# Four loads reordered, six dummy matmuls fewer and an uneven last output tile in a fused attention and expert kernel

## The chip, the core and the metric

The kernel runs on one core of a Trainium2 chip. A core has five engines with instruction streams of their own: TensorE (PE, the matrix multiplier; PEld is its weight load), VectorE (DVE), ScalarE (ACT), GpSimd (POOL) and SyncE (SP). They meet through semaphores. Transfers between device memory (HBM) and on-chip memory (SBUF) are issued by SP, ACT or POOL and carried out by 16 DMA engines, which all issuers share. Matmuls write to PSUM, a small accumulator memory in banks, from which DVE and ACT read.

The metric is the device time of one execution in microseconds (us). The profile is one execution recorded by the hardware; its *span* runs from the first to the last instruction.

## What is computed

Causal attention over 4 batches, 8 heads, 768 positions and head size 64, in which heads 0, 2 and 6 ("retrieval") see all earlier positions and the other five ("streaming") see the first 4 positions and a window of the last 64. Its output, 3072 rows of 512, goes through four experts, whose results are summed with normalised weights:

```python
scores = q @ k.T / 8;  a = softmax(where(mask[h], scores, -1e9))
x = (a @ v).transpose(0, 2, 1, 3).reshape(3072, 512)
p = probs / (probs.sum(-1, keepdims=True) + 1e-9)
out = sum(p[:, e:e+1] * (relu(x @ w1[e]) @ w2[e]) for e in range(4))
```

w1 is 4 x 512 x 1024 and w2 is 4 x 1024 x 512. All inputs are float32 in HBM; POOL's transfers turn them into float16 on the way.

## The kernel before, in words

**Groups and units.** The 3072 rows are cut into 8 groups of 384 (batch `b`, half `c`; `g = 2b + c`). For each group there is an attention (`attention(b, c)`, line 495) and four expert *units* (`moe_steps`, line 880). Unit (g, e) has two layers: layer 1 (line 895) multiplies w1(e) by the transposed attention output `xT[g]`, 8 x 4 matmuls of 384 columns, each finished block going through ReLU on ACT (line 908) into `hs`; layer 2 (line 919) multiplies `hs` by w2(e), 3 x 8 matmuls of 512 columns into `pO`, which DVE scales by `p_sb` and adds up in `acc` (lines 931 and 935). After the fourth expert SP writes `acc` out (line 940).

**Order of PE's work.** The order of the instructions on PE, DVE, ACT, POOL and SP is written out by hand. Attention of group 0 comes first, by itself; then the units of group g run with the attention steps of group g + 1 strewn among them, by planned costs (loop at line 968). An engine takes its instructions in that order; one that waits holds up all behind it.

**Group 0's attention** (lines 778 to 803). Head by head: transposes of q and k, scores (line 614), exp on ACT (line 632), and the values step. For streaming heads that is `values(h)` (line 709): its matmuls (line 726) take the loaded values `vS` as weights; then Ln and Exp on ACT (lines 744, 754 or 759) make the reciprocal of the softmax sum, and DVE multiplies it into `xT` (line 749). Heads 3 and 4 share one Exp. For retrieval heads `values_r` (line 647) is followed by DVE operations (lines 675 to 682) and, for head 6, by `x_transposes(6)` on PE (line 703) and a copy on DVE (line 707). The last steps are `values(5)`, `x_transposes(6)`, `values(7)`. Of `xT`'s four row blocks, block 1 holds heads 1 and 5, block 2 heads 2 and 6, block 3 heads 3 and 7; the first four blocks of layer 1 of unit (0, 0) use row blocks 0, 2 and 1 first and block 3 last (lines 886 to 907).

**Dummies.** `warm_up` (line 386) issues matmuls on a constant tile whose result nobody reads. In `values` (line 719) there are 4, 4, 6 and 10 of them, of 256 columns, ahead of heads 3, 4, 5 and 7.

**POOL's loads.** Every transfer that changes float32 to float16 is issued by POOL, in its program's order. The order up to line 483 is: values of group 0's heads, w1(0), values of heads 5 and 7, w2(0), w1(1), k and q of group 1 (`load_triples`), w2(1), retrieval values of group 1, w1(2), two of its streaming heads, w2(2), the other three, w1(3), w2(3). In between stand one-element copies, `landed(x)` (line 458): POOL waits there until x has arrived in SBUF. One w1(e) is two transfers of 512 KB and one w2(e) one of 1024 KB (sizes as they arrive); a head's values are 48 KB, k and q of group 1 are 384 KB each. POOL's transfers use eight semaphores in turn, so each also waits for the landing of the one eight before it. After w2(3), POOL clears some tiles and loads k (`kRr`, `kSr`), q and v of group 2.

**SP's queue.** For the groups from 2 on, q and k are transposed by DMA, issued by SP in `dma_transposes` (line 248), in order behind other work of SP: the first output (line 940), the copies of the first keys (lines 243, 244), three transposes of q (line 253), then `kR<-kRr` and `kS<-kSr` (line 259). PE's scores of group 2 need these.

**The last tile.** The last 128 rows of the last unit are written by `last_tile` (line 857) in two halves of 256 columns: 8 matmuls (line 863), one DVE operation (line 870) and one output transfer (line 875) each, the first transfer by SP, the second by ACT.

Of the kernel before, what the change touches and what calls it, by code (L numbers as in the profile page):

```python
# [17 lines left out]
def kernel(  # L18
# [33 lines left out]
    nc = tc.nc  # L52
    P = 128
    B, H, S, D = q.shape
    E, DM, F = moe_w1.shape
# [94 lines left out]
    def half(u):  # L150
        return slice(u * D, (u + 1) * D)
# [5 lines left out]
    def own_v(h):  # L157
        return half(PLACE[h][1])
# [10 lines left out]
    def v_tiles(b, c, h):  # L169

        if RETR[h]:
            return vR[b % 2][:, 3 * c : 3 * c + 3, RH.index(h), :]
        if b:
            return windows(vSf, c)[:, :, SH.index(h), :]
        return vS[:, c, :, SH.index(h), :]

    def v_tile(b, c, h, t):

        if b:
            return v_tiles(b, c, h)[:, t, :]  # L180
        return v_tiles(b, t // TC, h)[:, t % TC, :]
# [4 lines left out]
    def rows_of(x, b, h, c):  # L186
        return x[b, h, c * CH : (c + 1) * CH, :].rearrange("(j p) d -> p j d", p=P)

    def tiles_of(x, b, h, c):
        return x[b, h, c * CH : (c + 1) * CH, :].rearrange("(t r) d -> r t d", r=TK)  # L190

    def windows_of(x, b, h, c):

        assert b > 0
        first = ((b * H + h) * S + c * CH - WO) * D
        return bass.AP(x.tensor, x.offset + first, [[D, P], [WQ * D, WT], [1, D]])
# [13 lines left out]
    def load_triples(x, dst, b, c):  # L210

        gp.dma_start(
            out=dst.rearrange("p h j d -> p h (j d)"),
            in_=x[b, :, c * CH : (c + 1) * CH, :].rearrange(
                "h (p j) d -> p h (j d)", j=3
            ),
        )
# [47 lines left out]
    def load_v(b, c, heads):  # L265
        for h in heads:
            t = v_tiles(b, c, h)
            if RETR[h]:
                gp.dma_start(out=t[:, :, 0:D], in_=rows_of(v, b, h, c))  # L269
            elif b:  # L270
                gp.dma_start(  # L271
                    out=t[:, :, own_v(h)], in_=windows_of(v, b, h, c)
                )
            else:
                gp.dma_start(  # L275
                    out=t[R0:P, :, own_v(h)],
                    in_=tiles_of(v, b, h, c),
                )
# [18 lines left out]
    def load_w1(e, f0, f1):  # L297
        x = moe_w1[e].rearrange("(u c d) f -> u d c f", u=2, c=DMP)
        for u in range(2):
            gp.dma_start(  # L300
                out=w1sb[half(u), e * DMP : (e + 1) * DMP, f0:f1],
                in_=x[u, :, :, f0:f1],
            )

    def load_w2(e):
        gp.dma_start(
            out=w2sb[:, e * FTP : (e + 1) * FTP, :],
            in_=moe_w2[e].rearrange("(fo fi) d -> fi fo d", fi=P),
        )
# [41 lines left out]
    for h in range(H):  # L351
        if h == 2:
            nc.sync.dma_start(
                out=v_s32, in_=v[0, :, 0:NS, :].rearrange("h r d -> r h d")
# [13 lines left out]
        eng = nc.scalar if h < HP else nc.sync  # L368
        eng.dma_start(out=q32[:, :, h, :], in_=rows_of(q, 0, h, 0))
    nc.sync.dma_start(  # L370
        out=probs, in_=moe_domain_probs.rearrange("(t p) e -> p t e", p=P)
# [14 lines left out]
    def warm_up(ps, n, cols):  # L386
        for _ in range(n):
            nc.tensor.matmul(
                out=ps[:, 0:cols], lhsT=warm[:, 0:P], rhs=warm[:, 0:cols],
                start=True, stop=True,  # L390
            )
# [13 lines left out]
    def mask_s(x, n, keep, drop):  # L405

        gp.memset(x, keep)
        gp.affine_select(
            out=x, in_=x, compare_op=ALU.is_ge, fill=drop,
            base=R0, pattern=[[0, n], [1, TQ]], channel_multiplier=-1,  # L410
        )
        gp.affine_select(
            out=x, in_=x, compare_op=ALU.is_ge, fill=drop,
            base=NW - 1 - R0, pattern=[[0, n], [-1, TQ]], channel_multiplier=1,
        )
        gp.memset(x[0:R0, :, :], drop)
        gp.memset(x[0:NS, :, 0:TK], keep)
        gp.affine_select(
            out=x[0:NS, 0, 0:TK], in_=x[0:NS, 0, 0:TK], compare_op=ALU.is_ge,
            fill=drop, base=-NW, pattern=[[1, TK]], channel_multiplier=-1,  # L420
        )
# [23 lines left out]

    mask_c(bC, 0.0, -60000.0)
    mask_s(bS[:, 0:2, :], 2, 0.0, -60000.0)
    load_v(0, 0, [2, 1, 3, 4, 6])
    load_w1(0, 0, F)
    load_v(0, 0, [5, 7])  # L450
    load_w2(0)
    zero(gp, kR[0][:, 1, :, :, :])
    zero(gp, kS[:, 1, :, :, :].rearrange("p t s x -> p s t x"))
# [4 lines left out]
    def landed(x):  # L458

        gp.tensor_copy(out=seen, in_=x)  # L460
# [4 lines left out]
    def w2_of(e):  # L465
        return w2sb[0:1, e * FTP, 0:1]
# [2 lines left out]
    landed(w1_of(0))  # L469
    load_triples(k, k16, 0, 1)  # L470
    load_triples(q, qt16, 0, 1)
    landed(w2_of(0))
    load_w2(1)
    landed(qt16[0:1, 0, 0, 0:1])
    load_v(0, 1, RH)
    load_w1(2, 0, F)
    landed(w2_of(1))
    load_v(0, 1, SH[:2])
    load_w2(2)
# [12 lines left out]
    def mm_ns(cols):  # L492
        return cols / 2.4 + 2.5

    def attention(b, c):
# [213 lines left out]
        def values(h):  # L709
            if RETR[h]:  # L710
                yield from values_r(h)
                return
            ct, u = PLACE[h]
            if first and u == 1:
                ps = pO.tile([P, 512], FP32, name="pO", bufs=2)
            else:
                ps = pV.tile([P, 512], FP32, name="pV", bufs=2)
            if first:
                warm_up(ps, {3: 4, 4: 4, 5: 6, 7: 10}.get(h, 0), 256)
            work = []  # L720
            for es, parts in es_of[h]:
                for t, o, q0, nq in parts:
                    work.append((es, t, o, q0, nq))
            ns = 0
            for n, (es, t, o, q0, nq) in enumerate(work):
                nc.tensor.matmul(  # L726
                    out=ps[:, q0 : q0 + nq],
                    lhsT=v_tile(b, c, h, t),
                    rhs=es[:, o : o + nq],
                    start=(n == 0),  # L730
                    stop=(n == len(work) - 1),
                    skip_group_check=True,
                )
                ns += mm_ns(nq)
                if ns > 300 and n < len(work) - 1:
                    yield ns
                    ns = 0

            r, o = half(u), half(1 - u)
            pair = first and h in (3, 4)  # L740
            if not pair or u == 0:
                rc_of[0] = att.tile([P, CH], FP32, name="rc", bufs=4)
            rc = rc_of[0]
            nc.scalar.activation(  # L744
                out=rc[r, :], in_=ps[o, 0:CH], func=AF.Ln, bias=eps[o, :]
            )

            def scale(r=r, ps=ps):
                nc.vector.tensor_tensor(  # L749
                    out=xT[g][r, ct, :], in0=ps[r, 0:CH], in1=rc[r, :], op=ALU.mult  # L750
                )

            if not pair:
                nc.scalar.activation(out=rc[r, :], in_=rc[r, :], func=AF.Exp, scale=-1.0)  # L754
                later(scale)
            elif u == 0:
                scale_of[0] = scale
            else:
                nc.scalar.activation(out=rc, in_=rc, func=AF.Exp, scale=-1.0)
                later(scale_of[0])  # L760
                later(scale)

            yield ns + (600.0 if g == 1 else 0.0)
# [14 lines left out]
        if first:  # L778
# [8 lines left out]
            sink_row(5)  # L787
            sink_row(7)
            yield from both(scores(1), values(0))
            yield from transposes(2)  # L790
            yield from both(scores(3), values(2))
            x_transposes(0)
            yield from scores(4)
# [55 lines left out]
    def later(op):  # L849
        behind.append((clock[0] + LAG, op))  # L850
# [5 lines left out]

    def last_tile(e, nt, hs, acc):

        for n, eng in enumerate((nc.sync, nc.scalar)):
            cols = slice(n * DM // 2, (n + 1) * DM // 2)  # L860
            ps = pV.tile([P, 512], FP32, name="pV", bufs=2)
            for ft in range(FTP):
                nc.tensor.matmul(
                    out=ps[:, 0 : DM // 2],
                    lhsT=hs[:, ft, 2 * P : 3 * P],
                    rhs=w2sb[:, e * FTP + ft, cols],
                    start=(ft == 0),
                    stop=(ft == FTP - 1),
                )
            nc.vector.scalar_tensor_tensor(  # L870
                out=acc[:, cols], in0=ps[:, 0 : DM // 2],
                scalar=p_sb[:, nt, e : e + 1], in1=acc[:, cols],
                op0=ALU.mult, op1=ALU.add,
            )
            eng.dma_start(out=out[nt * P : (nt + 1) * P, cols], in_=acc[:, cols])


    acc = {}
# [157 lines left out]
```

The softmax here doesn't subtract the row's maximum and nothing guards it: scores larger than these inputs give would overflow.

## Time and profile before

| What | us |
|---|---|
| median of 4 executions | 399.31 |
| lowest and highest | 398.95, 399.71 |
| the profiled execution | 399.71 |
| its span | 397.9 |
| PE busy | 388.9 (98% of the span) |
| ACT busy | 219.2 (55%) |
| DVE busy | 156.4 (39%) |
| POOL busy | 143.7 (36%) |
| granted PE clock, mean | 1.000 |

A timeline row gives the start in us from the span's start, the time taken, the engine, the line of the kernel, the operation, what it writes and reads, and how many instructions are merged in the row; in square brackets stands the idle time of the engine just before it and what ended that. Rows of the waits say who waited for whom: us in total, how often, the longest. PE's matmuls overlap, so a row's time is longer than the distance to the next row; where costs are summed, that distance is used.

### The profile page before, as it was taken

To read this page: it belongs to the slowest core of one execution; us is meant where nothing else is said; L and a number is where in the kernel's file an instruction comes from. 1 tells how busy PE (TensorE), PEld (TensorE's weight loads), DVE (VectorE), ACT (ScalarE), POOL (GpSimd) and SP (SyncE) were. 2 spreads that over 40 slices of the span, in tenths; PEclk is the share of its full clock that TensorE was granted. 3 is DMA by queue.
4 is the path that set the end of the run, shared out by engine and by line. 5 is a ranking of instruction groups with operands and counts; after the bars stand their busy time and mean duration, and the time that the engine had idled before them with its cause. 6 is when DMAs were issued, how large, how long until landed. Compare 5 with 4: busy or idle time off the path is not lost.

```text
span 397.9 us, 7140 instructions
## 1 busy us (share of the span) xinstructions
PE 388.9 (98%) x2829; PEld 221.7 (56%) x2829; DVE 156.4 (39%) x344; ACT 219.2 (55%) x468; POOL 143.7 (36%) x184
## 2 busy tenths in 40 slices
PE   8899999989999999999999999999999999999996
PEld 5754556545555555555555555555555555655553
DVE  7734765324432334433342333433443223432222
ACT  3754569434766546655674446845564456853331
POOL 8833795808916905910039202950000000000000
PEclk9999999999999999999999999999999999999999
DMA  9999999999999999980779949990472000020002
GB/s 169 160 208 193 182 197 163 134 182 142 111 168 182 112 150 119 131 108 11 127 86 174 73 88 127 106 159 12 80 120 82 3 12 0 12 79 2 0 2 80
DMA packets 166133, 42.23 MB, mean 106 GB/s; under 512 B 156396, under 2 KB 161108, under 8 KB 166100
## 3 DMA queue, kind: packets, MB, share of 16 engines
q0 software_dynamic: 102656, 20.98, 62.8%
q1 hardware_dynamic: 61700, 20.27, 27.1%
q10 hardware_dynamic: 1744, 0.52, 0.6%
q8 instruction: 22, 0.36, 0.4%
q14 instruction: 11, 0.09, 0.1%
HBM read 43.57 MB, written 6.29 MB: 125 GB/s over the span
## 4 chain that ended last, share of the span: by engine, by line
PE 77%; DMA 15%; POOL 6%; issue 1%; DVE 0%; POOLq 0%
PE pA L895 35%; PE pO L919 35%; DMA w1sb<-in_moe_w_dram 4%; DMA w2sb<-in_moe_w_dram 4%; PE pA L614 4%; DMA q<-in_q_dram 3%; DMA kR<-kRr 2%; PE pV L726 1%; PE pV L662 1%; POOL vR L269 1%; DMA vS<-in_v_dram 1%; POOL q L201 1%; POOL w1sb L300 1%; POOL vS L275 1%; POOL vS L326 0%
## 5 line engine op out<-in xcount | busy, mean ns | idle before, releaser
L895 PE MATMUL pA<-xT,w1sb 128*128 128x384 f16 x1024 | 185.9, 326 | 0.1
L919 PE MATMUL pO<-w2sb,hs 128*128 128x512 f16 x760 | 179.0, 379 | 0.7 <-DMA w2sb<-in_moe_w_dram 0.7
L908 ACT ACTIVATE hs<-pA 128x384 f16<-128x384 f32 x256 | 122.0, 492 | 94.8 <-PE pA L895 89.5
L895 PEld LDWEIGHTS <-w1sb 128*128 128x128 f16 x1024 | 95.8, 98 | 59.6 <-issue 0.5
L919 PEld LDWEIGHTS <-hs 128*128 128x128 f16 x760 | 70.8, 98 | 73.7 <-DMA w2sb<-in_moe_w_dram 1.1
L632 ACT ACTIVATE es<-pA 128x384 f16<-128x384 f32 (+2 forms) x122 | 60.0, 511 | 54.5 <-PE pA L614 53.2
L935 DVE SCALAR_TENSOR_TENSOR acc<-pO,p_sb,acc 128x512 f32<-128x512 f32 x71 | 53.3, 750 | 71.7 <-PE pO L919 71.3
L227 POOL DMA_DIRECT2D kSr<-in_k_dram x30 | 30.1, 1007 | 31.5 <-DMA kS<-kSr 21.9
L223 POOL DMA_DIRECT2D kRr<-in_k_dram x18 | 14.1, 786 | 69.8 <-DMA kR<-kRr 69.7
L749 DVE TENSOR_TENSOR xT<-pV,rc 64x384 f16<-64x384 f32 x37 | 20.5, 554 | 32.0 <-ACT rc L754 24.3
L271 POOL DMA_DIRECT2D vS<-in_v_dram x30 | 30.5, 1026 | 0.2 <-DMA q<-in_q_dram 0.2
L931 DVE TENSOR_SCALAR acc<-pO,p_sb 128x512 f32<-128x512 f32 x24 | 18.0, 751 | 28.8 <-PE pO L919 28.6
L636 DVE TENSOR_TENSOR es<-es,mC 128x256 f16<-128x256 f16 (+1 forms) x42 | 10.9, 259 | 46.3 <-ACT es L632 45.3
L744 ACT ACTIVATE rc<-pV,eps 64x384 f32<-64x384 f32 x37 | 21.3, 576 | 12.0 <-PE pV L726 11.5
L614 PE MATMUL pA<-qT,kR 128*128 128x384 f16 (+2 forms) x120 | 24.5, 278 | 1.7 <-DMA kR<-kRr 1.1
L754 ACT ACTIVATE rc<-rc 64x384 f32<-64x384 f32 x38 | 19.8, 521 | 1.2
L269 POOL DMA_DIRECT2D vR<-in_v_dram x24 | 19.3, 804 | 0.4 <-issue 0.3
L614 PEld LDWEIGHTS <-kR 128*128 128x128 f16 x120 | 11.4, 98 | 11.7 <-DMA kR<-kRr 1.5
L636 DVE TENSOR_TENSOR es<-es,mW 128x384 f16<-128x384 f16 x30 | 10.7, 358 | 16.9 <-ACT es L632 16.8
L662 PEld LDWEIGHTS <-es 128*128 128x128 f16 x252 | 13.2, 97 | 7.2 <-ACT es L632 0.9
L726 PEld LDWEIGHTS <-vS 128*128 128x128 f16 x255 | 13.4, 98 | 6.8 <-DMA vS<-in_v_dram 1.2
L614 PEld LDWEIGHTS <-kS 128*128 128x128 f16 x255 | 13.3, 98 | 6.6 <-DVE kS L556 0.2
(102 smaller groups left out, 190.6 us busy)
## 6 DMA issues: line engine op xcount, KB each, us to landing
out_dram<-acc SPq DMA_DIRECT2D x23, 256.0 KB
w1sb<-in_moe_w_dram POOLq DMA_DIRECT2D x8, 512.0 KB, 9.7
w2sb<-in_moe_w_dram POOLq DMA_DIRECT2D x4, 1024.0 KB, 13.2
kSr<-in_k_dram POOLq DMA_DIRECT2D x30, 112.0 KB, 3.8
vS<-in_v_dram POOLq DMA_DIRECT2D x30, 112.0 KB, 5.7
q<-in_q_dram POOLq DMA_DIRECT2D x18, 128.0 KB, 4.6
vR<-in_v_dram POOLq DMA_DIRECT2D x24, 48.0 KB, 5.0
kRr<-in_k_dram POOLq DMA_DIRECT2D x18, 48.0 KB, 3.8
```

What stands on the lines that cost most here:

```text
L227: gp.dma_start(out=kSr[:, :, SH.index(h), own(h)], in_=windows_of(k, b, h, c),)
L269: gp.dma_start(out=t[:, :, 0:D], in_=rows_of(v, b, h, c))
L271: gp.dma_start(out=t[:, :, own_v(h)], in_=windows_of(v, b, h, c))
L614: nc.tensor.matmul(out=ps[:, o : o + nq], lhsT=key_tile(b, c, h, t), rhs=qTs[b, c][:, hp, q0 : q0 + nq], start=(n == 0 or not first), stop ...
L632: nc.scalar.activation(out=es[:, 0:cols], in_=ps[:, 0:cols], func=AF.Exp, scale=SC)
L636: nc.vector.tensor_tensor(out=es[:, o0:o1], in0=es[:, o0:o1], in1=m[:, mo : mo + o1 - o0], op=ALU.mult,)
L744: nc.scalar.activation(out=rc[r, :], in_=ps[o, 0:CH], func=AF.Ln, bias=eps[o, :])
L749: nc.vector.tensor_tensor(out=xT[g][r, ct, :], in0=ps[r, 0:CH], in1=rc[r, :], op=ALU.mult)
L895: nc.tensor.matmul(out=pss[ft][:, 0:CH], lhsT=w1sb[:, e * DMP + ct, ft * P : (ft + 1) * P], rhs=xT[g][:, ct, :], start=(n == 0), stop=(n = ...
L908: nc.scalar.activation(out=hs[:, ft, :], in_=ps[:, 0:CH], func=AF.Relu)
L919: nc.tensor.matmul(out=ps_o, lhsT=hs[:, ft, j * P : (j + 1) * P], rhs=w2sb[:, e * FTP + ft, :], start=(ft == 0), stop=(ft == FTP - 1),)
L935: nc.vector.scalar_tensor_tensor(out=acc[nt], in0=ps_o, scalar=p_ap, in1=acc[nt], op0=ALU.mult, op1=ALU.add,)
```

## The change

There are five edits; nothing else in the kernel differs.

1. In POOL's order, head 5's values of group 0 move from behind w1(0) to ahead of it.
2. `landed(w2_of(0))`, POOL's wait for w2(0), goes; w2(1) thus follows directly behind q of group 1.
3. w1(2) moves ahead of group 1's retrieval values.
4. Ahead of head 7's values there are 4 dummies in place of 10.
5. The last tile is cut into 384 columns (written out by SP) and 128 columns (by ACT) in place of 256 and 256.

```diff
-    load_v(0, 0, [2, 1, 3, 4, 6])
+    load_v(0, 0, [2, 1, 3, 4, 6, 5])
     load_w1(0, 0, F)
-    load_v(0, 0, [5, 7])
+    load_v(0, 0, [7])
     load_w2(0)
...
     load_triples(k, k16, 0, 1)
     load_triples(q, qt16, 0, 1)
-    landed(w2_of(0))
     load_w2(1)
     landed(qt16[0:1, 0, 0, 0:1])
+    load_w1(2, 0, F)
     load_v(0, 1, RH)
-    load_w1(2, 0, F)
     landed(w2_of(1))
     load_v(0, 1, SH[:2])
     load_w2(2)
...
-                warm_up(ps, {3: 4, 4: 4, 5: 6, 7: 10}.get(h, 0), 256)
+                warm_up(ps, {3: 4, 4: 4, 5: 6, 7: 4}.get(h, 0), 256)
...
-        for n, eng in enumerate((nc.sync, nc.scalar)):
-            cols = slice(n * DM // 2, (n + 1) * DM // 2)
+        for c0, c1, eng in ((0, 3 * P, nc.sync), (3 * P, DM, nc.scalar)):
+            cols = slice(c0, c1)
             ps = pV.tile([P, 512], FP32, name="pV", bufs=2)
             for ft in range(FTP):
                 nc.tensor.matmul(
-                    out=ps[:, 0 : DM // 2],
+                    out=ps[:, 0 : c1 - c0],
                     lhsT=hs[:, ft, 2 * P : 3 * P],
                     rhs=w2sb[:, e * FTP + ft, cols],
                     start=(ft == 0),
                     stop=(ft == FTP - 1),
                 )
             nc.vector.scalar_tensor_tensor(
-                out=acc[:, cols], in0=ps[:, 0 : DM // 2],
+                out=acc[:, cols], in0=ps[:, 0 : c1 - c0],
```

## The prediction

> **What bounds the kernel now.** I read the page first: engines, the slices, then the waits of PE.
>
> ```profile
> PE 388.9 (98%) x2829; PEld 221.7 (56%) x2829; DVE 156.4 (39%) x344; ACT 219.2 (55%) x468; POOL 143.7 (36%) x184
> ...
> PE   8899999989999999999999999999999999999996
> ...
> DMA  9999999999999999980779949990472000020002
> ```
>
> PE is busy 98% of the span, so the time is PE's work plus PE's few waits. The DMA row says the other half: for its first 17 slices, some 170 us, the DMA engines have no room. PE's waits, all of them:
>
> ```profile
> PE pO L388 <- DVE warm L373: 1.3, 1, 1.3
> PE pA L614 <- DMA kR<-kRr: 1.1, 1, 1.1
> PE pO L726 <- DMA vS<-in_v_dram: 0.9, 1, 0.9
> PE pV L662 <- ACT es L632: 0.8, 1, 0.8
> PE pO L919 <- DMA w2sb<-in_moe_w_dram: 0.7, 1, 0.7
> PE pA L614 <- ACT qT L525: 0.4, 1, 0.4
> ```
>
> Together 5.2 us, and the timeline puts the last of them at 86.69; after it PE never waits. The change can therefore act only on the 0.9 (head 5's values), the 0.7 (w2(1)), the 1.1 (`kR`), on dummies and on the tail. In the timeline of PE:
>
> ```profile
> 18.80 0.82 PE L388 MATMUL pO<-warm 128*128 128x256 f16 x6
> 20.54 0.42 PE L726 MATMUL pO<-es,vS 128*128 128x160 f16 x4 [0.92 <-DMA vS<-in_v_dram]
> 20.80 0.33 PE L703 MATMUL pV<-ident,x_pair 128*128 128x128 f16 x3
> 20.97 1.25 PE L388 MATMUL pO<-warm 128*128 128x256 f16 x10
> 22.06 0.41 PE L726 MATMUL pO<-es,vS 128*128 128x160 f16 x4
> ...
> 39.94 1.04 PE L919 MATMUL pO<-w2sb,hs 128*128 128x512 f16 x4 [0.71 <-DMA w2sb<-in_moe_w_dram]
> ```
>
> The two DMA waits follow each other, 19 us apart: whoever arrives earlier at 39.94 without an earlier w2(1) only waits longer there. So the question is when w2(1) lands, and POOL's timeline answers it, because its `landed` copies end when a transfer has arrived:
>
> ```profile
> 20.37 0.18 POOL L460 COPY seen<-w1sb 1x1 f16<-1x1 f16 x1 [1.83 <-DMA w1sb<-in_moe_w_dram]
> ...
> 25.45 0.18 POOL L460 COPY seen<-w2sb 1x1 f16<-1x1 f16 x1 [3.06 <-DMA w2sb<-in_moe_w_dram]
> 25.90 0.88 POOL L306 DMA_DIRECT2D w2sb<-in_moe_w_dram  x1 [0.28 <-issue]
> 34.59 0.18 POOL L460 COPY seen<-q 1x1 f16<-1x1 f16 x1 [7.82 <-DMA q<-in_q_dram]
> ...
> 40.01 0.18 POOL L460 COPY seen<-w2sb 1x1 f16<-1x1 f16 x1 [1.42 <-DMA w2sb<-in_moe_w_dram]
> ```
>
> What landed between these copies: to 25.45, w2(0), 1024 KB in 5.1 us with two 48 KB loads; to 34.59, w1(1), k and q, 1792 KB in 9.1 us; to 40.01, w2(1), 1024 KB in 5.4 us. That is 220, 196 and 189 KB per us: one full pipe, emptied in the order of issue. The windows view agrees: 210, 201 and 184 GB/s in 20 to 26, 26 to 35 and 35 to 40. w2(1) was issued at 25.90 but its turn came only when q was through, at 34.5. It stood 8.6 us in line.
>
> **Part by part.** The sum goes against the profiled execution, 399.71 us (span 397.9 and 1.8 around it), which is the slowest of four and 0.4 above their median of 399.31.
>
> *Head 5 ahead of w1(0).* Its issue (0.68 us, a third of the row of three such at 7.50, 2.05) now precedes w1(0). The queue is behind at that point (the loads issued at 8.88 and 9.54 land at 14.80 and 15.09), so nothing runs dry; w1(0) lands one load later, 20.32 becoming 20.49 (before, head 5 landed 0.17 after w1(0), head 7 another 0.17 later, at 20.66, where it stays). Head 5 lands at about 15.3. `values(5)` needs no wait and starts at 19.6. What is late next is head 6: DVE has `x_pair` ready at 20.10 (row of line 682: 19.74 and 0.36), so the transposes start at 20.15 in place of 20.80, not 0.92 earlier.
>
> *Six dummies fewer.* Ten took 20.97 to 22.06, 0.109 each. Four from 20.32 end at 20.76; head 7's values landed at 20.66, so `values(7)` starts there and layer 1 at 21.01 in place of 22.31: 1.30 earlier. What the dummies hid shows now: head 5's Ln, Exp and scale end 2.2 us after the start of `values(5)` (20.54 to 22.72 before), now at 21.8; the third matmul of layer 1, due at 21.34, needs them: 0.45 lost. Head 7's chain (2.17 from 22.06) ends at 22.93, ahead of the 13th matmul. Net 0.85 to 1.3 earlier; I take 1.0.
>
> *w2(1) directly behind q.* Removes one copy (0.18) and POOL's wait of 3.06; the issue moves from 25.90 to 22.4. POOL has nothing else to issue in between; behind it stands only the wait for q, which ends at 34.59 as before. In the queue w2(1) has the same transfers ahead of it: w1(0), heads 5 and 7, w2(0), w1(1), k, q. It lands at 39.9, as before. PE arrives at layer 2 of unit (0, 1) at 39.23 - 1.0 = 38.2 and waits 1.7 instead of 0.7. **Gain 0.** From here on PE is where it was.
>
> *w1(2) ahead of three loads.* POOL issues it at 35.0 (before 37.31), so the three loads land behind it. It lands at about 45.3 in place of 46.4 (the three took 40.0 to 40.9), but PE wants it only at 48.05: nothing. The three land at about 46.3; the first user is the row of line 662 at 48.70. POOL's eight semaphores shift: in the changed order the last three streaming loads wait for w1(2)'s halves, so w1(3) goes out at some 47.1 to 47.3 instead of 46.95. The queue then holds w2(2), which lands at 53.4: hidden. Everything up to w2(3) (landed at 65.0) is the same set of transfers, so group 2's loads, and the `kR` wait at 86.69, stay.
>
> *Tail.* Matmuls: 8 x 0.1625 (5.20 for 32 at line 895) and 8 x 0.0575 (by the line through 0.110 for 256 columns and 0.1625 for 384) make 1.76, as before (16 x 0.110). DVE: 0.75 for 512 and 0.48 for 256 columns give 0.62 and 0.35. The first part's matmuls end 0.43 later and DVE takes 0.13 longer: its transfer, now 192 KB, is issued 0.56 later. DVE ends the second part at 395.06 instead of 395.02; its transfer is 64 KB instead of 128, whose packets ran from 395.92 to 396.49. Bounds: -0.25 (half of the 0.57, if the small one ends last) to +0.56 (if the big one does and all its delay counts). Both share the engines and carry 256 KB together as before; I take +0.2.
>
> [...]
>
> **Sum.** 399.71 + 0 + 0.2 = 399.9 for an execution like the profiled one; the median stands 0.4 lower: **399.5**.
>
> **Rivals.** *As forecast (66%)*: the front's 1.0 is eaten at w2(1); 398.6 to 400.1, by the tail's bounds and the spread of four runs.
>
> *w2(1) does land earlier (20%, faster).* For it: 189 KB per us is the slowest of the three stretches, at 220 it would land 0.7 earlier, and if the faster of the four runs are those with an early w2(1), an earlier PE cashes that. Against: no gap in the queue. Price: at most 1.0 + 0.7 = 1.7, if w2(1) is there at 38.2. The `kR` wait follows: SP's transposes stand behind the first output, issued at 71.94 after PE's unit (0, 3), so they move with PE as long as group 2's k (landed at 70.2) is there. 399.5 - 1.7 = 397.8; half of it, 398.6.
>
> *The clock drops (7%, slower).* PE's first eight dummies took 3.59 us for what later takes 1.73 (8 x 0.216): half speed. If the wait of 1.7 us at 38.2 brings that back, it costs some 1.9 (those eight) to 2.6 (half speed from 1.26 to 6.47, where the clock's record begins to show full): 401.4 to 402.1. It decides from a wait longer than what the trace shows to be harmless: 0.76 and 0.92 idle between 17.69 and 20.54, with full clock in the page's PEclk row.
> [...] No row here has so long a wait after the start.
>
> *w2(1) lands later (7%, slower or same)*: w1(2)'s large packets, not the three small loads, now run beside the last of w2(1) on engines that are done early. Nothing shows it; 0.3 to 1.0, hence up to 400.5.
>
> **Numbers.** Faster by over 0.2% 0.21, within 0.2% 0.66, slower 0.13; 0.2%, 0.8 us, is about what a measurement of this kernel can tell from no change. The range, 397.9 to 400.3, takes in nearly all of the early w2(1) and leaves out the clock's drop and the worst of the late w2(1).
>
> **What would show it.** Right: PE's wait for `vS` gone, the one for w2(1) grown to 1.5 to 2.0 and ending at 39.9 again, `kR` still about 1.1. Wrong: the wait for w2(1) at or under 0.7 with a start before 39.2; a PEclk digit under 9 near 40; an output landing over 0.5 later.

## The result and the profile after

The changed kernel takes 400.57 us (median of 49 executions, 398.69 to 401.40), the kernel before 399.39 us beside it (72 executions, 398.10 to 402.25). The ratio is 1.0019, 95% interval 1.0011 to 1.0026: slightly slower, by an amount that lies at the edge of what can be told from no change. It is not the quotient of the medians (1.0030); the means, 400.22 and 399.46, have the same ratio of 1.0019.

The median hides two clusters. Each of 50 executions of the changed kernel has a record of PE's granted clock:

| Mean granted clock | Executions | Median us | Lowest, highest |
|---|---|---|---|
| 0.999 or 1.000 | 18 | 399.1 | 398.7, 400.1 |
| 0.996 | 32 | 400.75 | 400.4, 401.4 |

The clusters are 1.65 us apart, and 0.004 x 399 is 1.6 us: the lower clock accounts for the distance. The profiled execution (398.96, span 397.2) belongs to the upper row, so what it shows is the change *without* the loss. PE's waits in it:

```profile
PE pO L918 <- DMA w2sb<-in_moe_w_dram: 1.9, 1, 1.9
PE pO L388 <- DVE warm L373: 1.3, 1, 1.3
PE pV L661 <- ACT es L631: 0.8, 1, 0.8
PE pA L613 <- ACT qT L524: 0.4, 1, 0.4
PE pV L702 <- DVE x_pair L681: 0.3, 1, 0.3
PE pA L894 <- DVE xT L748: 0.2, 1, 0.2
```

The wait for head 5's values is gone, two small ones (head 6's `x_pair`, head 5's scale in `xT`) have come, and the wait for w2(1) has grown from 0.7 to 1.9. The lines have moved up by one. The timeline of PE, front and second unit:

```profile
19.70 0.41 PE L725 MATMUL pO<-es,vS 128*128 128x160 f16 x4
20.39 0.34 PE L702 MATMUL pV<-ident,x_pair 128*128 128x128 f16 x3 [0.28 <-DVE x_pair L681]
20.57 0.60 PE L388 MATMUL pO<-warm 128*128 128x256 f16 x4
21.01 0.41 PE L725 MATMUL pO<-es,vS 128*128 128x160 f16 x4
21.26 0.49 PE L894 MATMUL pA<-xT,w1sb 128*128 128x384 f16 x2
...
40.30 1.04 PE L918 MATMUL pO<-w2sb,hs 128*128 128x512 f16 x4 [1.87 <-DMA w2sb<-in_moe_w_dram]
```

Layer 1 begins at 21.26 instead of 22.31, and layer 2 of unit (0, 1) at 40.30 instead of 39.94: everything gained in the front has been waited away. POOL's timeline says why:

```profile
22.68 0.90 POOL L306 DMA_DIRECT2D w2sb<-in_moe_w_dram  x1
35.06 0.18 POOL L460 COPY seen<-q 1x1 f16<-1x1 f16 x1 [11.48 <-DMA q<-in_q_dram]
...
40.38 0.18 POOL L460 COPY seen<-w2sb 1x1 f16<-1x1 f16 x1 [1.35 <-DMA w2sb<-in_moe_w_dram]
```

w2(1) is issued 3.2 us earlier and arrives no earlier: 5.3 us after q, as before (5.4).

### The profile page after: what moved, and what is told of

Same layout as the page of the kernel before. It is cut to its first block, busy times and chain, and to the rows that moved or that the text cites. A ratio compares the mean times of both kernels' runs of the same rounds, so it can differ in the third digit from the quotient of the medians.

```text
span 397.2 us, 7125 instructions
## 1 busy us (share of the span) xinstructions
PE 388.4 (98%) x2823; PEld 220.9 (56%) x2823; DVE 156.7 (39%) x344; ACT 219.0 (55%) x468; POOL 143.4 (36%) x183
## 4 chain that ended last, share of the span: by engine, by line
PE 89%; DMA 7%; POOL 3%; issue 0%; DVE 0%; DVEq 0%; POOLq 0%
PE pO L918 40%; PE pA L894 39%; PE pA L613 5%; DMA w2sb<-in_moe_w_dram 4%; DMA w1sb<-in_moe_w_dram 2%; PE pV L725 2%; PE pV L661 2%; POOL vS L275 1%; POOL vR L269 1%; POOL bS L412 0%; PE pV L862 0%; PE pA L515 0%; POOL k L212 0%; POOL q L212 0%; DVE acc L869 0%
## 5 line engine op out<-in xcount | busy, mean ns | idle before, releaser
L223 POOL DMA_DIRECT2D kRr<-in_k_dram x18 | 14.1, 786 | 69.7 <-DMA kR<-kRr 69.7
L613 PE MATMUL pA<-qT,kS 128*128 128x55 f16 (+4 forms) x255 | 16.6, 195 | 0.0
```

Source lines behind the costliest of these rows:

```text
L613: nc.tensor.matmul(out=ps[:, o : o + nq], lhsT=key_tile(b, c, h, t), rhs=qTs[b, c][:, hp, q0 : q0 + nq], start=(n == 0 or not first), stop ...
```

## Experiments

Theory after the result: the front's gain makes the wait for w2(1) long enough for PE's clock to drop to half for one stretch in most executions. Rivals: the thinner dummies bring the drop themselves; edits 2 and 3 (the order of loads) or the uneven tile cost the time. Each kernel was timed beside the kernel before. "Over 400.2" counts executions above that time, a bound between the clusters of the changed kernel; with the kernel before there were 6 of 72 in the runs of the result, and 5 of 35, 4 of 35, 1 of 29 and 0 of 15 in those with a median of 399.05, 399.31, 399.20 and 399.54. These ratios, too, are not quotients of the medians.

| Kernel | Median us | Before, same chip | Ratio, 95% interval | Over 400.2 |
|---|---|---|---|---|
| changed + dummies in the wait | 399.35 | 399.05 | 1.0003 (0.9990 to 1.0015) | 0 of 12 |
| changed, 10 dummies again | 399.66 | 399.05 | 1.0020 (1.0003 to 1.0037) | 5 of 12 |
| before, w2(1) later | 401.49 | 399.05 | 1.0043 (1.0025 to 1.0061) | 10 of 12 |
| before + tile (5) | 399.01 | 399.05 | 0.9992 (0.9977 to 1.0007) | 0 of 12 |
| before + loads and tile (2, 3, 5) | 399.26 | 399.31 | 0.9999 (0.9980 to 1.0019) | 2 of 12 |
| before + front (1, 4) | 400.35 | 399.31 | 1.0018 (1.0004 to 1.0033) | 8 of 12 |
| changed + steps, lasting | 400.28 | 399.31 | 1.0012 (0.9985 to 1.0039) | 6 of 12 |
| before + steps, lasting | 401.27 | 399.31 | 1.0054 (1.0029 to 1.0078) | 9 of 12 |
| changed + steps once | 398.97 | 399.20 | 0.9981 (0.9968 to 0.9994) | 1 of 12 |
| before + steps once | 398.68 | 399.20 | 0.9987 (0.9977 to 0.9997) | 0 of 11 |
| changed, again | 400.83 | 399.20 | 1.0039 (1.0025 to 1.0053) | 10 of 12 |
| changed + steps once, kR later | 398.24 | 399.54 | 0.9970 (0.9960 to 0.9981) | 0 of 10 |

### Is it the wait, or the front? Dummies in the wait, dummies back, a longer wait alone

Dummies in the wait (changed kernel):

```diff
                 ps_o = pO.tile([P, DM], FP32, name="pO", bufs=2)
+                if (g, e, j) == (0, 1, 0):
+                    warm_up(ps_o, 8, 512)
```

> The changed kernel with 8 dummies of 512 columns (8 x 0.216 = 1.73 us) put between the two layers of unit (0, 1), where PE waits 1.87 us for w2(1). Theory: of the 49 executions of the changed kernel, 32 show a mean granted clock of 0.996 and lie at 400.75, 17 show 0.999 or 1.0 and lie at 399.1; the long wait lets the clock drop. With PE kept busy there: no execution under 0.999, median 399.0 to 399.4, the wait for w2(1) in the profile at 0.1 to 0.4. Rival (the thinner dummies ahead of head 7, at 19 to 22 us, bring the drop): two executions of three still at 0.996, median 400.4 to 400.8.

Measured: 399.06 to 400.01, no upper cluster and no clock under 0.998 (four executions show 0.998; a half-speed stretch behind PE's last matmul, as in the profile of before + steps, lasting, with its mean of 0.998, would give that). The front with its 4 dummies is untouched, so the thinner dummies are not the cause by themselves. The timeline shows the filler, and that w2(1) came late this time (landed 41.04), so that 1.0 of wait was left and not 0.1 to 0.4:

```profile
38.21 1.89 PE L388 MATMUL pO<-warm 128*128 128x512 f16 x8
41.09 1.02 PE L920 MATMUL pO<-w2sb,hs 128*128 128x512 f16 x4 [0.99 <-DMA w2sb<-in_moe_w_dram]
```

Ten dummies again (changed kernel):

```diff
-                warm_up(ps, {3: 4, 4: 4, 5: 6, 7: 4}.get(h, 0), 256)
+                warm_up(ps, {3: 4, 4: 4, 5: 6, 7: 10}.get(h, 0), 256)
```

> The changed kernel with 10 dummies ahead of head 7 again. PE comes 0.65 later to layer 2 of unit (0, 1) and waits 1.2 to 1.4 for w2(1). Theory: the drop becomes rare, under one execution of four at 0.996; median 399.2 to 399.7. Rival (the thinner dummies bring the drop by themselves): no drop at all, median 399.1 to 399.4.

Measured: seven executions at 398.8 to 399.7, five at 400.7 to 401.7. The drop came without thin dummies, against the rival, but more often than I expected: in the profiled execution w2(1) landed at 40.86, PE was there at 38.67, only 0.24 later than in the changed kernel and not 0.65, and the wait was 2.2, not 1.2 to 1.4:

```profile
40.91 1.89 PE L918 MATMUL pO<-w2sb,hs 128*128 128x512 f16 x4 [2.24 <-DMA w2sb<-in_moe_w_dram]
```

A longer wait with the front of before:

```diff
     landed(w2_of(0))
+    load_v(0, 1, RH)
     load_w2(1)
     landed(qt16[0:1, 0, 0, 0:1])
-    load_v(0, 1, RH)
     load_w1(2, 0, F)
```

> The kernel before, with group 1's three retrieval loads (1.03 us in the queue) ahead of w2(1); its front, with 10 dummies and head 5 behind w1(0), stays. w2(1) lands at 40.9, PE waits 1.6 to 1.8 instead of 0.71. Theory: the wait alone brings the drop, a third to two thirds of the executions at 0.996 and some 1.6 above the others, median 399.8 to 401.2. Rival (thinner dummies): no drop, 399.4 to 400.4, all of it the later w2(1).

Measured: no edit of the change is in this kernel, and ten of twelve lie over 400.2, seven of them, with a clock of 0.996, at 401.4 to 402.3. The wait in its profile is 3.0 (w2(1) landed at 41.68, later than I had worked out), with a half-speed stretch from 42.08 to 45.49. The wait alone is enough to bring the drop; the three executions at 400.25 to 400.7 have a full clock, and only the later w2(1).

```profile
41.73 1.58 PE L919 MATMUL pO<-w2sb,hs 128*128 128x512 f16 x4 [2.96 <-DMA w2sb<-in_moe_w_dram]
```

The changed kernel itself, once more, beside other kernels:

> The changed kernel itself, beside the two others on the same chip. Theory: two clusters again, near 399.1 and near 400.7, the upper one with a third to three quarters of the executions.

Measured: two executions at 399.2 and 399.6, ten at 400.6 to 402.7, more than expected. This time an execution with the drop was profiled (401.18, clock 0.996). Its page, its PE timeline and its windows (columns: stretch, length, busy time of PE, PEld, DVE, ACT and POOL, granted clock, DMA share, GB/s):

```profile
PE   7897999999999999999999999999999999999996
...
PEclk9999899999999999999999999999999999999999
```

```profile
40.74 1.04 PE L918 MATMUL pO<-w2sb,hs 128*128 128x512 f16 x4 [3.08 <-DMA w2sb<-in_moe_w_dram]
```

```profile
37.50:41.00 3.50, 0.42 (x4) 0.14 (x3) 0.50 (x1) 0.74 (x3) 1.59 (x3) 1.00 1.18 213
41.00:44.50 3.50, 3.50 (x22) 1.38 (x21) 2.33 (x4) 0.00 (x0) 2.96 (x4) 0.68 1.38 192
44.50:48.00 3.50, 3.50 (x21) 1.96 (x20) 1.71 (x4) 1.99 (x5) 2.65 (x5) 0.83 1.47 150
```

The fifth digit of PEclk is 8; the windows place it behind the wait, 0.68 and 0.83 where the profile of the change without the drop has 1.00. PE is "busy" all through, but issues 22 matmuls in 3.5 us, against 30 there. The trace's own record gives half speed from 42.28 for 3.413 us: 1.7 us lost.

### Which edits? Tile alone, loads and tile, front alone

The tile edit alone in the kernel before (its diff is the last hunk of the change):

> The kernel before with the uneven last tile alone (384 and 128 columns). Theory and rival alike: no drop of the clock; +0.1 to +0.2 by the profiles (from the first matmul of the last tile to the span's end 5.34 before, 5.46 after), 399.4 to 399.7. If the tail carries the loss instead: +0.7 or more.

Measured: no effect that shows (0.9992, interval 0.9977 to 1.0007). Loads and tile, edits 2, 3 and 5, with the front of before:

> The kernel before with edits 2, 3 and 5 (w2(1) directly behind q, w1(2) ahead of three loads, the uneven tile); its front stays. Theory: w2(1) lands when it did, so PE waits for it about as long as before (0.7 to 1.1); median 398.8 to 399.4, as the kernel before, with as few executions over 400 as that has. If issuing w2(1) 3.5 us earlier brought it earlier: no wait for w2(1), 398.2 to 398.6.

Measured: no effect that shows (0.9999; the interval, 0.9980 to 1.0019, is as wide as the effects in question). The wait for w2(1) did not go; in the profile it is 1.5, more than the 0.7 to 1.1 expected. The front, edits 1 and 4:

> The kernel before with edits 1 and 4 alone (head 5's values ahead of w1(0), 4 dummies ahead of head 7). Theory: PE comes a good 0.7 earlier to a w2(1) that lands as before, waits 1.5 to 2.2 and over 40% of the executions lose one half-speed stretch of 3.4 us, 1.6 us: median 399.8 to 400.8, upper cluster 400.4 to 401.4. If the loss needs edits 2 or 3: as before, 398.8 to 399.3.

Measured: 1.0018, eight of twelve at 400.25 to 400.9, all eight with a clock of 0.996; the front alone brings as much loss as the whole change. In its profiled execution PE waited 2.1 for w2(1) and the clock did *not* drop, which the next section explains:

```profile
40.45 1.04 PE L919 MATMUL pO<-w2sb,hs 128*128 128x512 f16 x4 [2.14 <-DMA w2sb<-in_moe_w_dram]
```

### Why only in some executions

In these profiles the record of the clock changes only on a grid of 3.413 us, which lies differently in each execution: the record of full clock lasts 392.533 us in the profile before and 389.119 in the changed kernel's first, 115 and 114 times 3.4133, and starts 6.47 and 6.99 us into the span (4.1 to 7.2 over all profiles). I laid that grid over each of the 14 profiles and added up PE's idle time per stretch, to 90 us. The stretch with the most:

| Profile | Most idle stretch, us | Idle in it, us | Drop at its end |
|---|---|---|---|
| w2(1) later | 38.67 to 42.08 | 2.96 | yes |
| 10 dummies again | 37.31 to 40.73 | 2.06 | yes |
| changed, again | 38.86 to 42.28 | 1.88 | yes |
| changed, first profile | 37.71 to 41.13 | 1.87 | no |
| before + steps once | 18.50 to 21.92 | 1.79 | no |
| before + front | 36.40 to 39.81 | 1.50 | no |
| before | 16.71 to 20.12 | 1.26 | no |

All others lie at or under 1.63 without a drop. So up to 90 us all 14 agree with one bound near 1.9 us of idle in one stretch, 55% of it: a drop at 1.88 and above, none at 1.87 and below. The length of the wait alone doesn't decide: the front-only kernel's wait of 2.14 was cut in two by the grid (1.50 and 0.64) and brought no drop, nor did one of 2.26 for `kR` (1.42 and 0.85, "changed + steps, lasting"), while 2.24, of which 2.06 lay in one stretch, did ("10 dummies again"). This explains how a wait of about 2 us can cost 1.65 in some executions and nothing in others.

The bound isn't sharper than about 0.1. Behind PE's last matmul the same count gives a drop at 2.10, 2.50 and 2.58 and none at 1.80, 1.84 and 1.96, and the last of these is over the 1.88 that brought a drop at 42.28; the profile models the ends of matmuls. Nor does every low mean clock go with a long time: one execution of the tile alone shows 0.994 at 399.55, and three of the kernel before 0.994 or 0.995 at 399.5 to 400.1. None of these was profiled, so why they lost so little is open.

### Filling the wait with work

If the wait is the loss, work put into it should turn the change into a gain. Two transposes and four score steps of group 1 (1.3 us of PE) were moved ahead of layer 2 of unit (0, 1):

```diff
+            more = 2250.0 if g == 0 and spent > 1.28 * UNIT else 0.0
-            while done < (spent - begin) / (end - begin) * att_ns:
+            while done < (spent - begin) / (end - begin) * att_ns + more:
```

> The changed kernel with six attention steps of group 1 (two transposes, four score steps, some 1.3 us of PE's work) moved ahead of layer 2 of unit (0, 1), into the wait for w2(1). Theory: the wait shrinks from 1.9 to 0.4 to 0.9, no drop of the clock, and the front's gain is kept: median 397.7 to 398.6. Rival (the gain is lost further on, at w2(2) or at kR, or PE now waits for DVE's copies of the transposes): no drop either, but 398.9 to 399.3.

> The kernel before with the same six attention steps moved ahead of layer 2 of unit (0, 1). Theory: its wait of 0.7 to 1.1 goes, PE is ahead by that much, its few executions over 400 go as well: median 398.2 to 398.8, 0.4 to 0.8 slower than the changed kernel with these steps. Rival: 398.9 to 399.3, as the wait for kR at 86.69 grows by what is gained.

Measured: five of twelve at 397.6 to 398.3, as the theory has it, but seven at 400.1 to 402.2, and the kernel before with the steps mostly slower, up to 404.4. Five of these seven, and four of the nine of the kernel before over 400.2, have a clock of 0.999 or 1.000, so in these the loss is another one. In the profiled execution of the first (400.45) the clock didn't drop; PE waited 2.3 us for `kR`:

```profile
87.22 0.39 PE L613 MATMUL pA<-qT,kR 128*128 128x128 f16 x2 [2.26 <-DMA kR<-kRr]
```

There w2(3) landed at 68.55 (64.40 in the changed kernel). The transpose `xT<-x_one` was issued at 48.11 (51.93 there), and w1(3)'s first half landed 7.1 us after w2(2), at 60.78 (3.5 us after it there, at 56.25). With the lead the whole rest of group 1's attention moves, and the supposition is that its transposes hold up the weights. To test that, the same steps without the lead: `spent > 1.28 * UNIT` becomes `1.28 < spent / UNIT < 1.4`.

> The changed kernel with the six attention steps of the earlier run ahead of layer 2 of unit (0, 1), but without the lasting lead: the steps after them wait until the plan has caught up, so from 47 us on PE's order is that of the changed kernel again, and the transposes xT<-x_one and xT<-x_pair stand where they stood. Theory: the wait for w2(1) is 0.4 to 0.9 and the clock does not drop; the upper cluster (400 to 402) of the lasting lead came from the transposes running into the weights' loads, and is gone: median 397.6 to 398.6, ten of twelve under 399. Rival (PE's lead as such is lost, at kR, whenever the loads are a bit late): the upper cluster stays in a third or more of the executions, median 398.8 to 400.5.

> The same steps, without the lasting lead, in the kernel before. Theory: its wait for w2(1) of 0.7 to 1.1 goes, 398.3 to 398.9, its few executions over 400 go. Rival: 399.0 to 399.4, with the wait for kR grown by what was gained.

Measured: 0.9981 and 0.9987, both faster than the kernel before; one execution over 400.2 in 23. So the upper cluster belonged to the lasting lead; that it is the transposes in it that hold up the weights was argued from one trace, not isolated. The spread of the changed kernel with steps, 397.6 to 400.2, is wider than expected (six of twelve under 399, not ten), and its median of 398.97 is over the 397.6 to 398.6 expected. Beside it the kernel before with the same steps takes 398.68: with the steps in the wait, the five edits bring no gain that shows, against the theory that the front's gain is kept. The slowest execution of the changed kernel with the steps was profiled:

```profile
87.01 0.39 PE L613 MATMUL pA<-qT,kR 128*128 128x128 f16 x2 [1.95 <-DMA kR<-kRr]
```

In this execution PE is early at `kR` and waits 1.95 us there. The last kernel puts 1.3 us of layer 1 in front of that wait:

```diff
-        begin = {0: 1.15, 1: 1.0}.get(g, 0.0) * UNIT
+        begin = {0: 1.15, 1: 1.15}.get(g, 0.0) * UNIT
```

> The changed kernel with the six attention steps ahead of layer 2 of unit (0, 1), as in the run before, and with group 2's first scores, which wait for kR, eight matmuls (1.3 us) later in PE's order (the plan for group 1 begins at 1.15 units instead of 1.0). Theory: what is left of the loss stands at kR (1.9 us of wait in the last profile); with 1.3 us of layer 1 in front of it the wait falls to 0 to 1.0, median 397.7 to 398.6, the executions closer together. Rival (the lead is lost anyway, kR or a later load moves with it): 398.7 to 399.2, spread as before.

Measured: 398.24 (397.86 to 398.56), ratio 0.9970, interval 0.9960 to 0.9981, the best and the steadiest of all. The kernel before with both additions was not run, so how much of this is owed to the five edits isn't shown. `kR` no longer ends a wait; what is left is 1.1 at w2(1):

```profile
40.57 1.67 PE L918 MATMUL pO<-w2sb,hs 128*128 128x512 f16 x7 [1.08 <-DMA w2sb<-in_moe_w_dram]
...
84.03 2.11 PE L894 MATMUL pA<-xT,w1sb 128*128 128x384 f16 x12
86.06 0.39 PE L613 MATMUL pA<-qT,kR 128*128 128x128 f16 x2
```

## Why the prediction was right or wrong, point by point

**Right: the front's gain is eaten at w2(1).** Layer 2 of unit (0, 1) starts at 40.30 after a wait of 1.87, which the prediction put at 1.7. PE got there at 38.43 instead of 39.23, 0.8 earlier (I took 1.0), though its front ran 0.25 later in this execution from 18.80 on. Head 5's scale cost 0.23 of the 0.45 foreseen; `x_pair` is the new wait, 0.28, as said. With dummies in the wait and no drop of the clock, which is the case that the sum describes, the ratio is 1.0003 (0.9990 to 1.0015): gain 0.

**Right: issuing w2(1) earlier brings nothing.** Loads and tile alone give 0.9999, but an interval of 0.9980 to 1.0019 would hold a gain of 0.7 us too; the landings decide, 5.3 to 5.9 us behind q in all eight profiles with the earlier issue. With the same transfers ahead of it w2(1) took 17.6 us from issue to landing, and 14.1 from issue to POOL's copy in the profile before (25.90 to 40.01).

**Wrong: the clock.** The sum has the clock at nothing and leaves its drop to a rival with 7%, and this rival decided two executions of three. I let it decide "from a wait longer than what the trace shows to be harmless", and that trace had no wait over 1.1 once the clock was full. That a wait of 1.7 leaves the clock at full speed, as the sum has it, was my assumption; no run had shown it. What the runs show instead: a wait near 1.9, 55% of one stretch of 3.413 us, is enough when nearly all of it falls into one (1.88 us in one stretch brought the drop, 1.87 did not). The rival's price, 1.9 to 2.6, was too high: one stretch at half speed, 1.65 between the clusters. The sign that was named for being wrong, a PEclk digit under 9 near 40, stands in the page of the profile with the drop.

**The number: near, with luck.** The median of 400.57 is 1.1 above the 399.5 forecast, and over the range of 397.9 to 400.3. The ratio of 1.0019 lies just inside "within 0.2%", which had 0.66, and on the 399.31 of before it gives 400.1, inside the range. That is luck in part: no cluster is where the forecast puts the kernel. Executions without the drop lie at 399.1, 0.3 under the kernel before, and those with it at 400.75, 1.4 over it; the ratio averages the two.

**Undervalued (7%): w2(1) lands later.** From q's landing to w2(1)'s took 5.3 to 5.9 us (mean 5.6) in the eight profiles with edits 2 and 3, and 5.0 to 5.4 (mean 5.1) in the five with the order of before. So the wait also grows from its far end by about 0.5. Whether the earlier issue or w1(2) beside its last packets does that wasn't separated; the rival's 0.3 to 1.0 was an estimate that no row gave.

**Not held: the wait for `kR` stays at 1.1.** The changed kernel's first profile has none (w2(3) landed 0.6 earlier than in the profile before). Over all profiles it is 0 to 2.3, so a single profile doesn't give it.

**Tail.** +0.2 was forecast; the profiles, from the tile's first matmul to the span's end, give 5.34 and 5.46; the tile alone gives 0.9992, with an interval (-0.9 to +0.3 us) that holds both 0 and +0.2.

## What to carry to other kernels

Before shortening what stands ahead of a transfer that PE waits for, look up when that transfer can land at all: here it stood in a full queue, and the 0.8 us gained ahead of it became idle time: the wait for it was 1.87 us in place of 0.71, with 0.36 of the growth from a later landing. Idle time is not free: when 1.88 to 2.96 us of it fell into one 3.413 us stretch here, PE's clock dropped to half for the next, and an edit that saved nothing then cost 1.65 us, in some executions and not in others. What helped here was to fill the gap with real work that has its inputs, moved there without moving what follows it, and then to give the next wait down the line room as well.

## What had not been expected of the hardware

In the first 90 us PE's clock dropped to half at the end of a 3.413 us stretch with 1.88, 2.06 or 2.96 us of PE idle, and did not at 1.87 or less; behind the last matmul one stretch with 1.96 idle brought no drop. It came back after exactly one stretch in each of the three. Waits of 2.14 and 2.26 us that straddled two stretches brought no drop. The same transfer, w2(1), landed between 39.8 and 41.1 us in executions whose queue ahead of it held the same loads.
